# A feed-forward layer in two phases: the whole first product through DRAM, then the second, both in the seven-product form

## The chip, the cores and the metric

One core of a Trainium2 chip runs the whole program. The metric is the device time of one execution in microseconds, as the median of several runs; lower is better. A profiled execution gives, beside it, the span from the first to the last instruction and a trace of every instruction.

## The reference, cut to what matters

Causal attention over 4 batches, 12 heads, 448 positions and head size 64 makes x of 4 x 448 rows and 768 columns. A Fourier mix is added, the rows are normed, and two products with a ReLU between them make the feed-forward layer:

```python
X = np.fft.fft(np.fft.fft(x, axis=1), axis=2)
u = x + np.real(X)
un = (u - mean(u)) / np.sqrt(var(u) + 1e-06)
ch = np.maximum(un @ w_ch1, 0.0) @ w_ch2     # 768 -> 3072 -> 768
return u + ch
```

## The kernel before, in words

The work is cut into units by `tile_kernel`. Each unit has an engine (or a choice of engines), a cost, a priority and the tiles that it reads and writes. `Plan.order` is a list scheduler in Python: it always takes the unit that can start first by its own model, and so writes out one fixed order for every engine. The table `LEADS` shifts the priority of single units. All DMAs are issued by SyncE, in that order. Tiles live in pools ("A1", "A2", "Q", "E1", "E2", "L") that share memory: a pool opens when those named in `AFTER` have seen their last use.

Attention (`attend`, 24 pairs of heads) and the Fourier part (`fold`, `dft`, by batch) come first. `dft` writes u to the DRAM tensor `ud` and the transposed, normed un to `und`.

The 1792 rows of un form two groups of 896 (two batches each), and the 3072 middle columns 12 chunks of 256. An item is one group and one chunk; the 24 items run group by group. For each, `f1` makes the first product for the chunk and `f2` adds the second one to the sums `acc0` to `acc6`, which stay in SBUF for the whole group. The `f1` of one item and the `f2` of the item before it are interleaved on TensorE.

Every factor is split into a high and a low fp32r part, and a product takes three matmuls: high by high, high by low, low by high. A 2 x 2 product of blocks takes eight block products in the plain form, and seven in the other form (named `fast` for `f1`, `seven` for `f2`), which needs sums and differences of blocks first (`mixed`, `halves`, `quarters`, `hblocks`).

- `f1`, matmuls of 128x448: the items of group 0 with chunk 0 to 2 are plain (4 outputs, 18 matmuls each: 72). The other 21 items take 7 products of 9 matmuls (63).
- `f2`, matmuls of 128x384: ten items of group 0 are plain (line 1484: 7 row tiles, 2 halves, 6 matmuls: 84). The other fourteen, chunks 4 and 6 of group 0 (`STR`) and all of group 1, are seven-product (line 1445: 7 steps x 3 row tiles x 3 matmuls, and 12 matmuls for the seventh, middle row tile that has no partner: 75).

After each product of three matmuls (six in a plain item) VectorE adds the PSUM bank to `acc` (line 1433). In the seven-product form a bank runs through several steps, and the next step in it waits for that addition. In `f1` a pass runs through seven products, copies three of them to `c` tiles (`keep`, line 611), adds on VectorE (`plus`, line 1314) and applies ReLU (line 1263).

Weights are read in `weights` with their layout of bits undone by three ScalarE operations (lines 989, 993, 1006) and two of VectorE (1012, 1016) per 128 rows; `halves` and `quarters` split them (high part line 611, low part 1066 and 1126). Group 1 reads `w1` parts that group 0 left in DRAM (`wp`).

## Time and profile before

| | us |
|---|---|
| median of 3 runs | 899.98 |
| lowest and highest | 898.37, 901.57 |
| span of the profiled execution | 896.1 |
| median less span | 3.9 |
| TensorE busy in the profile | 879.0 |

The page of the profile gives each engine's busy time over the span; a table of stretches gives the same for chosen parts of it, also for the instructions of one line alone. The durations of matmuls in the trace overlap, since they are pipelined.

### The profile page before, as it was taken

Reading aid. Unit: us, or ns where it says so; the run is one execution under the profiler, and the core shown is the slowest. Engines: PE = TensorE matmul, PEld = TensorE weight load, DVE = VectorE, ACT = ScalarE, POOL = GpSimd, SP = SyncE. Lnnn points to the kernel's source line nnn. Section 1 sums busy time; section 2 is a strip of 40 time slices with the busy share of each in tenths; the row PEclk is TensorE's granted clock in tenths of the full one; section 3 lists DMA queues with packets and bytes.
Section 4 is the critical chain, followed back from the end, with each engine's and each line's share of the span. In section 5 each row is a group of like instructions: output and inputs, shape, how many; then the busy total and the mean of one; then the engine's idle time right before and its main releaser. Section 6 shows DMA issues by size and latency. Waiting matters only on the chain.

```text
span 896.1 us, 15887 instructions
## 1 busy us (share of the span) xinstructions
PE 879.0 (98%) x5560; PEld 785.3 (88%) x5560; DVE 682.1 (76%) x1281; ACT 595.1 (66%) x1258; POOL 512.2 (57%) x596
## 2 busy tenths in 40 slices
PE   8999999999999999999999999999999999999998
PEld 4676686676889999999999999999999999999998
DVE  5868979868987988999999888867535445755748
ACT  6889998958675887989877568554534334544452
POOL 1564645735323230313135223889997969899996
PEclk9999999999999999999999999999999999999999
DMA  6456656324589565876698685764363344244113
GB/s 253 137 166 200 183 192 190 113 68 130 169 276 324 195 270 199 291 286 244 230 343 316 242 269 179 272 230 148 106 211 119 132 141 152 93 125 157 37 53 124
DMA packets 70081, 169.52 MB, mean 189 GB/s; under 512 B 19184, under 2 KB 31984, under 8 KB 70000
## 3 DMA queue, kind: packets, MB, share of 16 engines
q1 hardware_dynamic: 70000, 168.50, 56.1%
q8 instruction: 44, 0.72, 0.3%
q14 instruction: 37, 0.30, 0.1%
HBM read 112.63 MB, written 55.84 MB: 188 GB/s over the span
## 4 chain that ended last, share of the span: by engine, by line
PE 76%; DVE 10%; POOL 5%; ACT 4%; DMA 3%; issue 2%; SPq 0%; DVEq 0%; ACTq 0%; POOLq 0%
PE psum L1240 29%; PE psum L1445 17%; PE psum L1484 14%; PE psum L779 4%; PE psum L713 4%; PE psum L789 4%; PE psum L850 2%; DVE acc L1433 2%; ACT p L733 1%; DVE mn L725 1%; PE psum L706 1%; DVE w L1016 1%; DMA us<-und 1%; POOL w L1137 1%; PE psum L938 1%
## 5 line engine op out<-in xcount | busy, mean ns | idle before, releaser
L1433 DVE TENSOR_TENSOR acc<-psum,acc 128x384 f32<-128x384 f32 x462 | 243.9, 553 | 100.1 <-PE psum L1445 83.4
L1484 PE MATMUL psum<-w2h,hh 128*128 128x384 f32 x280 | 94.5, 338 | 0.9 <-ACT us L1263 0.6
L1006 ACT ACTIVATE w<-w 128x768 int8<-128x768 f32 x48 | 94.3, 1964 | 0.4
L1484 PE MATMUL psum<-w2l,hh 128*128 128x384 f32 x280 | 94.4, 337 | 0.0
L1484 PE MATMUL psum<-w2h,hl 128*128 128x384 f32 x280 | 94.2, 337 | 0.0
L733 ACT ACTIVATE p<-psum,mn 128x128 f32<-128x128 f32 (+3 forms) x168 | 82.8, 518 | 12.7 <-DVE mn L725 8.3
L1033 POOL TENSOR_TENSOR w2l<-w,w2h 128x768 fp32r<-128x768 f32 x20 | 40.3, 2026 | 74.4 <-ACT w2h L1029 63.8
L1445 PE MATMUL psum<-w2h,hh 128*128 128x384 f32 x336 | 73.0, 338 | 0.0
L1445 PE MATMUL psum<-w2l,hl 128*128 128x384 f32 x336 | 70.2, 339 | 0.1
L725 DVE TENSOR_REDUCE mn<-psum 128x1 f32<-128x448 f32 (+3 forms) x96 | 61.4, 665 | 10.9 <-PE psum L713 10.6
L767 POOL TENSOR_TENSOR p<-p,ri 128x128 f32<-128x128 f32 (+3 forms) x62 | 34.1, 572 | 62.3 <-DVE ri L745 52.4
L1314 DVE TENSOR_TENSOR c<-psum,c 128x448 f32<-128x448 f32 x63 | 38.7, 617 | 39.1 <-PE psum L1240 27.4
L713 PE MATMUL psum<-raw,qs 64*128 64x128 f32 (+3 forms) x336 | 66.6, 430 | 1.6 <-DMA cd<-in_cd_dram 1.1
L1445 PEld LDWEIGHTS psum<-w2h,hh 128*128 128x128 f32 x336 | 60.5, 188 | 1.4
L1445 PEld LDWEIGHTS psum<-w2l,hl 128*128 128x128 f32 x336 | 59.7, 188 | 1.6 <-DVE acc L1433 0.4
L779 PEld LDWEIGHTS psum<-cst,p 128*128 128x128 f32 x384 | 42.5, 141 | 19.8 <-issue 9.4
L1240 PE MATMUL psum<-u12h,w 128*128 128x448 f32 x162 | 59.3, 368 | 0.2 <-DVE acc L1433 0.2
L1240 PE MATMUL psum<-u21h,w 128*128 128x448 f32 x162 | 59.2, 368 | 0.1
L1240 PE MATMUL psum<-u11h,w 128*128 128x448 f32 x162 | 58.8, 368 | 0.2 <-DVE w L1066 0.2
L1240 PE MATMUL psum<-u22h,w 128*128 128x448 f32 x162 | 58.7, 368 | 0.0
L611 ACT CAST w2h<-w 128x384 fp32r<-128x384 f32 x56 | 28.4, 513 | 45.5 <-PE psum L1445 22.9
L779 PE MATMUL psum<-cst,p 128*128 128x128 f32 x384 | 52.8, 278 | 3.5 <-POOL p L767 2.3
(171 smaller groups left out, 2526.9 us busy)
## 6 DMA issues: line engine op xcount, KB each, us to landing
...
us<-und SPq DMA_DIRECT2D x45, 224.0 KB, 4.1
...
```

Of the source, the lines that this page charges most:

```text
L713: nc.tensor.matmul(out=T[ps][:, at[r]:at[r] + n], lhsT=T[qs][s, q0:q0 + 128], rhs=T[raw][s, QW:QW + n], start=False, stop=y == len(rows) - ...
L725: nc.vector.tensor_reduce(out=z, in_=x, axis=AX, op=ALU.min)
L733: nc.scalar.activation(out=T[pb][:, PO[rr]:PO[rr] + n], in_=T[ps][:, c0:c0 + n], func=ACTF.Exp, scale=-1.0, bias=T[mn][:, rr:rr + 1], accu ...
L779: nc.tensor.transpose(T[ps][:, 128 * k:128 * k + 128], T[pb][:, e:e + 128], T["cst", 0][:, 0:128])
L789: nc.tensor.matmul(out=T[xps][64 * h:64 * h + 64, q0:q0 + w], lhsT=T[v][:, c, h * D:(h + 1) * D], rhs=T[pa][:, s0 + h * sd:s0 + h * sd + w ...
L1006: nc.scalar.activation(out=T[w].bitcast(I8)[:, :, 3], in_=T[w][:, :, 1].bitcast(F32), func=ACTF.Prelu, scale=SIGN_SCALE, alpha=SIGN_ALPHA)
L1033: nc.gpsimd.tensor_tensor(out=T[wl], in0=T[w32].bitcast(F32), in1=T[wh], op=ALU.subtract)
L1240: nc.tensor.matmul(out=T[ps][:, 0:S], lhsT=a[:, t], rhs=x[:, t], start=start and k == 0, stop=stop and k == 8, skip_group_check=True)
L1314: nc.vector.tensor_tensor(out=T[z], in0=T[ps][:, 0:S], in1=T[z], op=ALU.add)
L1433: nc.vector.tensor_tensor(out=x, in0=T[ps][:, 0:384], in1=x, op=ALU.add)
L1445: nc.tensor.matmul(out=T[ps][:, 0:384], lhsT=hpart(j, h, a)[:, k * 128:k * 128 + 128], rhs=T[z][:, 384 * b:384 * b + 384], start=start and ...
L1484: nc.tensor.matmul(out=T[ps][:, 0:384], lhsT=T[a][:, m, k * 128:(k + 1) * 128], rhs=w[:, sl], start=(m == 0 and z == 0), stop=(m == 1 and ...
```

## The change

The feed-forward layer no longer runs item by item. First all of the first product runs, and its ReLU output goes to a DRAM tensor `h`; then the second product runs, and reads `h` back.

- First phase: chunks 0 to 2 for group 0 alone (`ALONE`), chunks 3 to 11 for both groups step by step in turn, then chunks 0 to 2 for group 1 alone, with w1 read again from DRAM. Every pass is in the seven-product form: 24 passes of 63 matmuls.
- Second phase: a window is one pair of row tiles, tile i of group 0 with tile i of group 1, and three chunks (`WIN`): 7 steps of 9 matmuls that sum over the three chunks in one PSUM bank before VectorE adds the bank to the sum. There are 7 x 4 = 28 windows. The sums of all 14 row tiles stay in SBUF.
- The pieces of w2 are made once for each chunk, 7 of the 12 chunks in the first phase (`EARLY`), which go to DRAM and come back (`fetch`).
- The U blocks of group 0 are mixed while attention still runs (`build`): u11 and u21 stay in SBUF tiles of their own (`EDGE`), the others go through DRAM (`td`) and are split in `refill`. The U blocks of group 1 are built in a pool that opens after "Q".
- Buffers: 3 `p` buffers of attention (4 before), 2 `w` (3), 5 `w32` (4), 8 `w1` tiles (7), 4 `us` (5). PSUM: up to 4 banks for each group's first product and 8 for the second (5 and 5 before).
- A new table `PICK` fixes the engine of many units, and `LEADS` has new values throughout.

```diff
-N_RAW, N_V, N_QK, N_W, N_W32, N_PA, N_RB = 4, 4, 2, 3, 4, 2, 2
+N_RAW, N_V, N_QK, N_W, N_W32, N_PA = 4, 4, 2, 2, 5, 2
 F1_CUT = 3
+ALONE, WIN, REST, EARLY, JOIN = 3, 3, (0,) * 7, (0, 3, 5, 6, 8, 9, 11), ()
+W1_LEAD, W1_LEAD2, W2_LEAD, H_LEAD, W2_FROM, W2_TILL, FETCH_LEAD = 1200, 1500, 2600, 600, 3000, 5000, 2000
+BUILD_AT = (19000, 300)
-BANKS = dict(sc=(1, 3), sd=(1, 2), pt=(1, 3), x=(1, 2), ay=(1, 3), an=(1, 1), at=(1, 5), h=(0, 5), o2=(0, 5))
-N_P, N_XT, N_Y, N_F, N_D = 4, 1, 1, 1, 1
-AFTER = dict(E1=("A1",), E2=("A1", "A2"), L=("Q",))
+BANKS = dict(sc=(1, 3), sd=(1, 2), pt=(1, 3), x=(1, 2), ay=(1, 3), an=(1, 1), at=(1, 5), h0=(0, 4), h1=(0, 4), o2=(0, 8))
+N_P, N_XT, N_Y, N_F, N_D = 3, 1, 1, 1, 1
+AFTER = dict(E0=("A1",), E2=("A1", "A2"), L=("Q",), F=("E2",), G=("L",))
+BELOW = dict(E2=("E0",))
...
+UB = ("11", "21", "t2", "t1", "t3", "22", "t4")
+W1B = ("11", "12", "s2", "s1", "s3", "s4", "22")
+W2B = ("11", "21", "t2", "t1", "t3", "22", "t4")
+HB = ("x0", "x1", "s2", "s1", "s3", "s4", "y1")
+STEPS = (
+    ("x0", "11", "a", 0, 0, True, False), ("x1", "21", "d", 0, 0, True, True), ("s2", "t2", "a", 0, 1, False, False),
+    ("s1", "t1", "b", 1, 1, True, False), ("s3", "t3", "a", 1, 1, False, False), ("s4", "22", "b", 0, 1, False, True),
+    ("y1", "t4", "a", 1, 0, False, True))
...
+    def build(g, p0):
+        ph = "E" if g else "Q"
+        for k in range(3):
+            p = p0 + (30 if g else 300) * k
+
+            def minus(name, x, y, rd=()):
+                plan.part("minus", g, k, name)
+                into = y if name in ("t1", "t3") else x
+                return combine(S, into[0], x, y, ALU.subtract, (*into[1][0][:2], name), p + 2, ph, rd)
+
+            def put(name, src):
+                if g or name in EDGE:
+                    return usplit(g, name, k, src, p + 3, ph)
+                plan.part("td", k, name)
+
+                def f(k=k):
+                    nc.sync.dma_start(out=dr["td"][UB.index(name)][:, k], in_=src[0]())
+                add("D", dma(229376), p + 3, f, rd=src[1], wr=[("td", name, k)], phase=ph)
+                return [("td", name, k)]
+            plan.part("slabs", g, k)
+            b11 = slab(g, 0, k, 1, p, ph)
+            b12 = slab(g, 1, k, 1, p, ph)
+            b22 = slab(g, 1, k + 3, 1, p, ph)
+            b21 = slab(g, 0, k + 3, 1, p, ph)
+            d11 = put("11", b11)
+            t1 = minus("t1", b12, b11, d11)
+            put("t1", t1)
+            d22 = put("22", b22) if g else []
+            t3 = minus("t3", b22, b12, t1[1])
+            put("t3", t3)
+            t2 = minus("t2", b22, t1, [*d22, *t3[1]])
+            put("t2", t2)
+            d21 = put("21", b21)
+            t4 = minus("t4", b21, t2, d21)
+            put("t4", t4)
...
+    FLOW = (
+        ("11", "11", "a", True, False), ("12", "21", "d", True, True), ("s2", "t2", "a", False, False), ("s1", "t1", "b", True, False),
+        ("s3", "t3", "a", False, False), ("s4", "22", "b", False, True), ("22", "t4", "a", False, True))
+    place = {c: k for k, c in enumerate([*range(ALONE, NCH), *range(ALONE)])}
+
+    def f1(c, gs, again, p0):
+        step = 143 * len(gs)
+        bank, kept = {}, {}
+        for s, (wn, un, x, first, last) in enumerate(FLOW):
+            for y, g in enumerate(gs):
+                plan.part("f1", c, g, s)
+                p = p0 + step * s + 143 * y
+                ps = ("h%d" % g, (c, x))
+                wb = ("w1", ((c, again), wn))
+                us = [utile(g, un, t) for t in range(3)]
+                dep = [] if first else [kept["u2", g][1]] if wn == "s3" else [kept["m1", g][1]] if wn == "s2" else \
+                    [kept["u3", g][2]] if wn == "s4" else [kept["u3", g][1]]
+                for q in range(F1_CUT):
+                    ks = range(9 * q // F1_CUT, 9 * (q + 1) // F1_CUT)
+                    ts = sorted({k // 3 for k in ks})
+
+                    def f(ks=ks, ps=ps, wb=wb, us=us, first=first, last=last):
+                        w = T[wb]
+                        for k in ks:
+                            t, z = divmod(k, 3)
+                            a, b = ((0, 0), (0, 1), (1, 0))[z]
+                            nc.tensor.matmul(
+                                out=T[ps][:, 0:S], lhsT=w[:, a, t], rhs=T[us[t]][:, b], start=first and k == 0, stop=last and k == 8,
+                                skip_group_check=True)
+                    add("PE", len(ks) * mm(S) + 19 / F1_CUT, p + q, f,
+                        rd=[(*wb, "h"), (*wb, "l"), *[(*us[t], z) for t in ts for z in "hl"], *dep,
+                            *([(*ps, s, q - 1)] if q else [])],
+                        wr=[(*ps, s, q)], phase="E")
+                done = (*ps, s, F1_CUT - 1)
...
+                def out_(z, key, m, n, p, g=g):
+                    def f():
+                        nc.sync.dma_start(out=dr["h"][m, g][:, place[c], n * S:(n + 1) * S], in_=T[z])
+                    add("D", dma(229376), p - 1500, f, rd=[key], wr=[("hd", m, g, c, n)], phase="E")
+
+                def keep(name, ps=ps, done=done):
+                    z = ("us" if again and name == "m1" else f"c{g}", (c, name, again))
+
+                    def f(eng):
+                        copy(eng, T[z], T[ps][:, 0:S])
+                    add(("S", "V"), (act(448), dve(448)), p + 143, f, rd=[done], wr=[(*z, 0)], phase="E")
+                    kept[name, g] = [z, (*z, 0)]
+
+                def plus(name, m, n, ps=ps, done=done):
+                    z = kept[name, g][0]
+
+                    def f():
+                        nc.vector.tensor_tensor(out=T[z], in0=T[ps][:, 0:S], in1=T[z], op=ALU.add)
+                    add("V", dve(448), p + 144, f, rd=[done, (*z, 0)], wr=[(*z, 1)], phase="E")
+                    kept[name, g].append((*z, 1))
+                    relu(z, lambda: T[z], [(*z, 1)], (acts(448), dve(448, 1.92)), m, n)
+
+                def relu(z, src, rd, cost, m, n):
+                    def f(eng):
+                        if eng == "S":
+                            nc.scalar.activation(out=T[z], in_=src(), func=ACTF.Relu)
+                        else:
+                            nc.vector.tensor_scalar(out=T[z], in0=src(), scalar1=0.0, scalar2=None, op0=ALU.max)
+                    add(("S", "V"), cost, p + 145, f, rd=rd, wr=[(*z, 2)], phase="E")
+                    out_(z, (*z, 2), m, n, p)
+
+                if wn == "11":
+                    keep("m1")
+                elif wn == "12":
+                    plus("m1", 0, 0)
+                elif wn == "s2":
+                    keep("u2")
+                elif wn == "s1":
+                    kept["b", g] = (ps, done)
+                elif wn == "s3":
+                    keep("u3")
+                    plus("u3", 1, 1, *kept["b", g])
+                elif wn == "s4":
+                    plus("u2", 0, 1)
+                else:
+                    z = (f"c{g}", (c, "c21", again))
+                    relu(z, lambda ps=ps: T[ps][:, 0:S], [done], (act(448), dve(448)), 1, 0)
...
+    def slice_(k, name):
+        return ("wa" if (7 * k + W2B.index(name)) % (N_WA + N_WB) < N_WA else "wb", (k, name))
...
+    def window(i, k0, k1, p0):
+        order = [*range(ALONE, NCH), *range(ALONE)]
+        n, id_ = k1 - k0, ("h", i, k0)
+        w = 128 * n
+        ns = sorted({(i * 128) // S, (i * 128 + 127) // S})
+        raw = {}
+        plan.part("raw", i, k0)
+        c, c_ = ("c0", "c1") if len(seen) == 1 else (f"c{len(seen) % 2}",) * 2
+        seen.append(id_)
+        for name, tag, m, g in (("y0", c, 0, 1), ("y1", c_, 1, 1), ("x0", "us", 0, 0), ("x1", "us", 1, 0)):
+            z = (tag, (id_, name))
+
+            def f(z=z, m=m, g=g):
+                nc.sync.dma_start(
+                    out=T[z][:, 0:w].rearrange("p (c t) -> p c t", c=n), in_=dr["h"][m, g][:, k0:k1, i * 128:i * 128 + 128])
+            add("D", dma(512 * w), p0 - 1000, f, rd=[("hd", m, g, order[k], q) for k in range(k0, k1) for q in ns], wr=[z], phase="L")
...
+        bank = {x: ("o2", (id_, x)) for x in "abd"}
+        for s, (h, wn, x, row, half, first, last) in enumerate(STEPS):
+            plan.part("f2", i, k0, s)
+            ps, hb, acc = bank[x], ("w1", (id_, h)), acc_(i + NT * row)
+            p = p0 + 94 * n * s
+            ws = [slice_(k, wn) for k in range(k0, k1)]
+
+            def f(ps=ps, hb=hb, ws=ws, first=first, last=last):
+                for y, z in enumerate(ws):
+                    for v, (a, b) in enumerate(((0, 0), (0, 1), (1, 0))):
+                        nc.tensor.matmul(
+                            out=T[ps][:, 0:384], lhsT=T[hb][:, a, y], rhs=T[z][:, b], start=first and y + v == 0,
+                            stop=last and y == n - 1 and v == 2, skip_group_check=True)
+            add("PE", 3 * n * mm(384) + 8, p, f, rd=[(*hb, "h"), (*hb, "l"), *[(*z, v) for z in ws for v in "hl"],
+                *([] if first else [(*ps, "v")])], wr=[(*ps, s)], phase="L")
+
+            def f(ps=ps, k=i + NT * row, half=half):
+                x = whole(k)[:, half * 384:(half + 1) * 384]
+                nc.vector.tensor_tensor(out=x, in0=T[ps][:, 0:384], in1=x, op=ALU.add)
+            add("V", dve(384) + 4, p + 94 * n, f, rd=[(*ps, s), (*acc, half)], wr=[(*acc, half), (*ps, "v")], phase="L")
...
+    at(-9000, build, 0, BUILD_AT[0])
+    at(-800, refill, F0 - 800)
+    at(BUILD_AT[1], build, 1, F0 + BUILD_AT[1])
+    for c in range(NCH):
+        t = 1000 * c if c < ALONE else 1000 * (2 * c - ALONE)
+        at(t - W1_LEAD - 200, w1s, c, False, F0 + t - W1_LEAD)
+        at(t, f1, c, (0,) if c < ALONE else (0, 1), False, F0 + t)
+        if c < ALONE:
+            t = 1000 * (2 * NCH - ALONE + c)
+            at(t - W1_LEAD2, w1s, c, True, F0 + t - W1_LEAD2)
+            at(t, f1, c, (1,), True, F0 + t)
+    t, last, gate = 2000.0 * NCH, [0] * NT, []
+    for k in range(NCH):
+        if k not in EARLY:
+            at(t - W2_LEAD, w2s, k, F0 + t - W2_LEAD)
+        else:
+            x = W2_FROM + (2000.0 * NCH - W2_TILL - W2_FROM) * EARLY.index(k) / len(EARLY)
+            at(x, w2s, k, F0 + x)
+            at(t - W2_LEAD, fetch, k, F0 + t - FETCH_LEAD + (30 * k if k < WIN else 0))
+        for i in range(NT):
+            if k == NCH - 1 or (k + 1) % WIN == REST[i]:
+                if not last[i]:
+                    for row in range(2):
+                        at(t - H_LEAD, total, i + NT * row, F0 + t, gate[-2:-1])
+                    gate.append((f"c{len(gate) % 2}" if len(gate) != 1 else "c0", (("h", i, last[i]), "y0")))
+                at(t - H_LEAD, window, i, last[i], k + 1, F0 + t)
+                t += 282 * (k + 1 - last[i])
+                if k == NCH - 1:
+                    for row in range(2):
+                        at(t - H_LEAD, store, i + NT * row, F0 + t)
+                last[i] = k + 1
+    for _, _, fn, args in sorted(todo, key=lambda x: x[:2]):
+        fn(*args)
```

## Rows read from the trace of the kernel before

**Rows 1.** The page: the span; busy time, share and instructions of each engine
```profile
span 896.1 us, 15887 instructions
PE 879.0 (98%) x5560; PEld 785.3 (88%) x5560; DVE 682.1 (76%) x1281; ACT 595.1 (66%) x1258; POOL 512.2 (57%) x596
```

**Rows 2.** Stretches: from:to, length, busy time of each engine (instructions), clock, DMA
```profile
227.00:300.00 73.00, 71.86 (x385) 65.50 (x384) 61.28 (x100) 48.99 (x75) 24.35 (x24) 1.00 0.74 248
300.00:475.00 175.00, 173.73 (x920) 164.92 (x919) 168.26 (x312) 149.31 (x216) 44.84 (x37) 1.00 0.74 265
300.00:875.00 575.00, 573.63 (x3053) 549.14 (x3052) 423.08 (x765) 353.16 (x628) 365.04 (x382) 1.00 0.57 194
```

**Rows 3.** The chain that ended last, in order of time: start, length, what
```profile
266.77 18.27 PE psum L1240 x90
...
485.89 24.98 PE psum L1484 x144
```

**Rows 4.** The same stretches, line 1240 alone (PE, PEld)
```profile
227.00:300.00 73.00, 47.44 (x216) 39.63 (x216) 1.00 0.74 248
300.00:475.00 175.00, 94.34 (x414) 76.77 (x415) 1.00 0.74 265
300.00:875.00 575.00, 297.86 (x1323) 245.48 (x1323) 1.00 0.57 194
```

**Rows 5.** The same stretches, line 1484 alone
```profile
227.00:300.00 73.00, 11.49 (x66) 11.62 (x67) 1.00 0.74 248
300.00:475.00 175.00, 67.17 (x356) 62.30 (x354) 1.00 0.74 265
300.00:875.00 575.00, 145.41 (x776) 136.26 (x774) 1.00 0.57 194
```

**Rows 6.** The same stretches, line 1445 alone
```profile
300.00:475.00 175.00, 31.24 (x150) 26.64 (x150) 1.00 0.74 265
300.00:875.00 575.00, 185.10 (x954) 169.60 (x955) 1.00 0.57 194
```

**Rows 7.** Groups of instructions: count, busy time, mean ns, idle time before
```profile
L1006 ACT ACTIVATE w<-w 128x768 int8<-128x768 f32 x48 | 94.3, 1964 | 0.4
L1016 DVE SCALAR_TENSOR_TENSOR w<-w,w 128x768 uint32<-128x768 uint32 x48 | 46.6, 973 | 3.0 <-ACT w L1006 2.8
L1314 DVE TENSOR_TENSOR c<-psum,c 128x448 f32<-128x448 f32 x63 | 38.7, 617 | 39.1 <-PE psum L1240 27.4 <-ACT c L611 11.1
L611 ACT COPY c<-psum 128x448 f32<-128x448 f32 x61 | 32.7, 542 | 34.4 <-PE psum L1240 29.6 <-POOL hh L1372 4.6
L1066 DVE TENSOR_TENSOR w<-w,w 128x384 fp32r<-128x384 f32 x37 | 24.5, 679 | 5.3 <-ACT w L611 5.2
L1066 POOL TENSOR_TENSOR w<-w,w 128x384 fp32r<-128x384 f32 x11 | 11.6, 1057 | 25.5 <-ACT w L611 16.5 <-DVE w L613 7.4 <-issue 1.6
```

**Rows 8.** Instructions of PE in order of time: start, length, what
```profile
227.01 0.47 PE L1240 MATMUL psum<-u11h,w 128*128 128x448 f32 x1
...
266.03 0.74 PE L938 MATMUL psum<-cst,un 112*128 112x112 f32 x6
```

**Rows 9.** DMA issues: count, KB each, median us from issue to landing
```profile
us<-und SPq DMA_DIRECT2D x45, 224.0 KB, 4.1
und<-ub SPq DMA_DIRECT2D x32, 168.0 KB, 3.0
```

**Rows 10.** Instructions of DVE in order of time: start, length, what
```profile
271.04 0.38 DVE L613 CAST t3h<-us 128x448 fp32r<-128x448 f32 x1
271.34 2.04 DVE L613 CAST t2h<-us 128x448 fp32r<-128x448 f32 x1
```

**Rows 11.** Instructions of POOL in order of time, the same moment
```profile
271.26 3.84 POOL L1033 TENSOR_TENSOR w2l<-w,w2h 128x768 fp32r<-128x768 f32 x2 [6.66 <-ACT w2h L1029]
```

**Rows 12.** The stretch from the start to 102.4, line 733 alone (ACT)
```profile
0.00:102.40 102.40, 43.95 (x169) 1.00 0.60 191
```

**Rows 13.** The stretch from the start to 99.4, line 779 alone (PE, PEld)
```profile
0.00:99.40 99.40, 22.13 (x163) 18.19 (x164) 1.00 0.59 190
```

1032 lines of the change are left out of this document (423 added, 609 removed), and 1791 rows, old and new, of tables (LEADS, PICK).

## The prediction

> **What bounds the kernel now.** The page comes first: TensorE is called busy for 98% of the span, every other engine for 57 to 76% [rows 1]. The durations behind that 98% overlap, so I read the true rate from the chain of waits in order of time, where long runs of one line stand unbroken: 90 matmuls of line 1240 in 18.27 us, 0.203 us each, and 144 of line 1484 in 24.98 us, 0.1735 us each [rows 3]. Line 1445 has the same shape and I give it the same price. Then the table of stretches, by line, shows how densely these stand. From 300 to 875 there are 1323 matmuls of 128x448 and 776 + 954 of 128x384 [rows 4 to 6], and no others, for the sum is the stretch's own count of 3053 [rows 2]. At those rates they need 268.6 + 300.2 = 568.8 of 575 us: 6.2 us, 1.1%, is lost. In the hardest part, 300 to 475, VectorE is busy for 168 of 175 us and ScalarE for 149 [rows 2], and 414 + 506 matmuls need 171.8 us [rows 4 to 6]: 3.2 us lost, 1.8%. So the feed-forward part is bound by the number of matmuls and by nothing else, even where two other engines are nearly full. The clock is 1.00, the 2.4 GHz level, in all three stretches [rows 2].
>
> The way into it is looser. The first matmul of line 1240 stands at 227.01, and the last of the Fourier part at 266.03 [rows 8]. From 227 to 300 there are 216 of line 1240 and 66 of line 1484 [rows 4, 5], 43.8 + 11.5 = 55.3 of 73 us. The other 17.7 us are 103 matmuls (385 less 282 [rows 2]) of the Fourier part, and waits.
>
> **The change part by part.** *First product.* Before: 3 items of 72 and 21 of 63 matmuls, 1539. After: 24 passes of 63, 1512. 27 x 0.203 = **5.5 us less**.
>
> *Second product.* Before: 10 items of 84 and 14 of 75, 1890. After: 28 windows of 63, 1764. 126 x 0.1735 = **21.9 us less**. That a bank now sums nine matmuls in place of three changes neither their number nor their shape. VectorE's additions fall from 462 to 196, but VectorE isn't on the path, so this is worth nothing by itself. It also loosens a wait: in a window, the step that reuses a bank has one whole step, 9 x 0.1735 = 1.56 us, between itself and the one whose sum VectorE must read first; before, s3 followed s2 in bank "a" with two products of three matmuls between, 1.04 us.
>
> *Density.* I let the 1.1% stand, so it is worth nothing either way. The lower bound is the whole 6.2 us given back; the upper one is the 1.8% of the hardest stretch for all 613 us of matmuls, 4.3 us more than now. The load of a two-group chunk (126 x 0.203 = 25.6 us) supports it: every chunk needs two halves of w1 and, for 7 of 12 chunks in that phase, w2 too, which the schedule spreads at about 0.9 w2 chunk per w1 chunk. That is 3.8 runs of the bit operations; the dearest takes 1.96 us on ScalarE and the dearest 0.97 us on VectorE [rows 7]. Some 21 low parts and differences at 0.68 us on VectorE or 1.06 us on GpSimd [rows 7], six copies at 0.54 us and six additions at 0.62 us [rows 7] come to less than 25.6 us on each engine if GpSimd takes half of the low parts.
>
> *The way in.* This is new work at a tight place. Let the 17.7 us of others stay as they are: three passes of group 0 alone are 189 x 0.203 = 38.4 us, so they end at 227 + 38.4 + 17.7 = 283.1, and group 0's pass of chunk 3 at 295.9. Group 1 needs its U blocks by then. They go into pool "L", which opens after the Fourier part. Its last matmul is at 266.8 [rows 8], the write of und lands 3.0 us later and a slab takes 4.1 us more [rows 9]: 273.9. There are 12 slabs and 4 buffers, so three rounds, each with one landing and a chain of some eight operations in series (split, t1, t3, t2, t4, split) at about 0.68 us: 4.1 + 5.4 = 9.5 us. The first product needs u11 of the third round, 273.9 + 2 x 9.5 + 4.1 + 1.4 = 298.4, 2.5 us after PE has run dry. Taken: **3 us more**. Bounds: below nothing by 4, if the two products on u11 and u21 (18 x 0.203 = 3.7 us) that need no new pool fill waits before 227; 15 us above, if the three rounds don't overlap with the refill of group 0, which takes 15 more slabs through the same four buffers (four landings of 4.1 us).
>
> *Attention.* The mixing of group 0 adds 12 differences, 12 halves of splits and DMAs to its last fifth; GpSimd is at 57% over the span [rows 1] and can hide them. The fourth `p` buffer goes. At the tightest place that I found, the thirteenth pair's first exponential has just begun at 102.4 (12 pairs of 14 instructions, and 1 [rows 12]) while the tenth pair's 16 transposes were over by 99.4 (163 of line 779, 160 are needed [rows 13]): with three buffers it would have been free. Taken: 0. Bounds: 4 us either way, as the engines are assigned anew.
>
> *Between the phases.* The windows begin with chunks 3 to 5, whose rows of `h` were written long before. 17 slices of w2 have a pool ("wa") that opens when group 0 is done, 38 us ahead. Only four blocks of the third slice must wait for the last matmul of the first phase; the first of them is needed after three steps, 4.7 us, and takes a high and a low part, about 0.7 + 1.06 us [rows 7]. Covered. SyncE's queue holds the raw reads of the next windows behind the fetches of w2; if one is late, it costs a landing, 4.1 us [rows 9]. Taken: **1 us more**, bounds 0 and 5. At the very end the last addition and the last store stay: 0.
>
> **Sum:** -5.5 - 21.9 + 3 + 1 = -23.4 us. The span of 896.1 becomes 872.7; the median lies 3.9 us above the span, so **876.6 us**.
>
> **The rivals.** *A shared port.* At 271.34 a cast on VectorE took 2.04 us where its twin took 0.38 [rows 10], while GpSimd had begun a two-input subtraction at 271.26, two of which took 3.84 us [rows 11]: one engine stood while the other worked. On the way in, low parts and differences of chunks 1 to 3 (33), of the refill (15) and of group 1 (33) stand in 227 to 296. If they never overlap between the two engines, they take 81 x 0.68 + 6 x 0.97 = 60.9 us when all are VectorE's, and 0.38 us more for each that GpSimd takes: 76 us at 40 of them. VectorE has the Fourier part's own work too and must give some away. About 76 us against 68.9 us of PE's work is 7 us more than forecast: **883 us**. The Trainium skill, "SBUF — State Buffer", section "Who interferes with whom", speaks against the change here: a VectorE instruction with two SBUF inputs and a GpSimd one that reads SBUF exclude each other. The cast above agrees as to exclusion. Against the rival: work for chunk 1 can stand before 227.
>
> *A lucky way in.* The 18 matmuls before 227, no wait for group 1 and none between phases: 876.6 - 3.7 - 3 - 1 = **869 us**.
>
> *The evacuation chain of the first phase (slower).* Within a pass, s3's bank is copied (0.54 us), b's bank is added to the copy (0.62 us) [rows 7], and only then may s4 go into b. In the two-group phase only the other group's product, 9 x 0.203 = 1.83 us, lies between, and the second product no longer stands there to fill. If ScalarE's queue has a 1.96 us operation and VectorE's a 0.97 us one in front [rows 7], the chain is 4.1 us and the pass loses 2.3 us, or all 4.1 in the six single-group passes: 18 x 2.3 + 6 x 4.1 = 66 us at worst. It turns the gain into a loss from 23.4 / 24 = 1 us for each pass; at half its worst, 33 us, the time is **910 us**. Against it: the same chain ran 21 times before beside a VectorE at 96%, with 1.8% lost in all; the t4 product needs only the copy; and each group has a fourth bank, so the next chunk's first product can step in.
>
> That the change doesn't do what it says can't be here: the counts follow from the loops.
>
> **How the numbers follow.** Forecast 0.56, shared port 0.18, lucky way in 0.14, evacuation chain 0.12, of which 0.07 is slower, 0.03 within 0.3% and 0.02 still faster. A measurement of this kernel can tell about 0.3% (2.7 us) from no change. So faster 0.90, same 0.03, slower 0.07. The range takes in 869 less the 4 us of attention and 883 with the 4.3 of density and the 5 of the phases: 865 to 892. It leaves out the worse end of the way in and most of the chain.
>
> **What would show it.** In the trace after: 1512 and 1764 matmuls at 0.203 and 0.1735 us; 196 additions into the sums; the first-product phase starting near 227 and its last matmul near 227 + 17.7 + 307 + 3 = 555; unbroken chains on TensorE in both phases. Wrong would be: waits of TensorE on copies in 300 to 550 (chain), VectorE and GpSimd operations at twice their price near 270 to 300 (port), attention that ends some us off 227, or any fall of the granted clock after a pause between the phases.

## The result and the profile after

| | before | after |
|---|---|---|
| median of 4 runs, us | 899.17 | 888.40 |
| lowest and highest | 897.56, 901.57 | 886.11, 891.54 |
| profiled execution, its span | 896.1 (span) | 887.22, 885.4 |
| forecast | | 876.6 (865 to 892) |

The ratio is 0.9884 (95% interval 0.9856 to 0.9912). The change is faster by 10.8 us, where 23.4 were forecast: the sign and the range held, and half of the gain is missing. The page of the profile after, first part (busy time and instructions of each engine), answers to [rows 1]:

```profile
PE 856.2 (97%) x5407; PEld 758.5 (86%) x5407; DVE 745.5 (84%) x1458; ACT 531.4 (60%) x1094; POOL 327.6 (37%) x355
```

In the file after, line 2802 makes the first product, 2979 the second, 2987 VectorE's additions to the sums, 2655 low parts, 2661 sums and differences of blocks, 2262 and 2264 copies and casts, 2461 to 2478 the Fourier fold, 2440 the last step of attention; in the files of the experiments the same lines stand some lines lower. The table of stretches after, all engines (columns: stretch, its length, busy time and count of PE, PEld, DVE, ACT, POOL, granted clock, DMA share, GB/s), beside [rows 2]:

```profile
0.00:227.00 227.00, 219.05 (x2019) 156.91 (x2021) 190.42 (x415) 194.06 (x556) 110.10 (x164) 0.98 0.58 186
227.00:300.00 73.00, 62.56 (x331) 52.99 (x332) 67.73 (x126) 57.27 (x105) 24.04 (x25) 0.98 0.64 200
300.00:525.00 225.00, 224.74 (x1101) 205.84 (x1100) 183.23 (x325) 170.84 (x242) 53.60 (x47) 1.00 0.81 273
525.00:575.00 50.00, 46.45 (x230) 42.05 (x229) 42.13 (x82) 33.95 (x55) 17.00 (x15) 1.00 0.76 250
575.00:612.00 37.00, 34.53 (x192) 32.81 (x192) 36.32 (x71) 15.62 (x30) 8.86 (x7) 1.00 0.86 285
612.00:882.30 270.30, 268.87 (x1543) 267.88 (x1541) 225.40 (x446) 59.62 (x108) 113.97 (x97) 1.00 0.44 140
```

and line 2802 alone in the first four of them (PE, PEld, clock, DMA share, GB/s):

```profile
0.00:227.00 227.00, 4.91 (x18) 3.00 (x18) 0.98 0.58 186
227.00:300.00 73.00, 47.19 (x199) 36.39 (x200) 0.98 0.64 200
300.00:525.00 225.00, 224.74 (x1101) 205.84 (x1100) 1.00 0.81 273
525.00:575.00 50.00, 41.22 (x198) 36.28 (x196) 1.00 0.76 250
```

Read them with the two rates of the forecast, 0.203 and 0.1735 us. From 300 to 525 there are 1101 matmuls, 223.5 of 225 us: 0.7% lost. From 612 on 1543 x 0.1735 = 267.7 of 270.3: 1%. Both phases are as dense as forecast. Three places are not. From 227 to 300 only 199 x 0.203 = 40.4 of 73 us are feed-forward work, where there were 55.3 before. From 525 to 575, 198 x 0.203 + 32 x 0.1735 = 45.7 of 50 (4.3 lost), and from 575 to 612, 192 x 0.1735 = 33.3 of 37 (3.7 lost). The waits of TensorE, from the list of waits (what it waited for: us in total, times, longest), say on what, first for 227 to 300 and then for 525 to 612:

```profile
PE psum L2802 <- DVE 0t L2655: 5.4, 3, 4.7
PE psum L2802 <- ACT c L2262: 1.4, 2, 0.8
PE psum L2802 <- DVE 1211_3676 L2655: 1.1, 1, 1.1
PE psum L2802 <- DVE w L2655: 0.9, 1, 0.9
PE psum L2802 <- DVE c L2264: 0.7, 1, 0.7
...
PE psum L2802 <- DVE c L2264: 1.9, 1, 1.9
PE psum L2802 <- ACT c L2262: 1.7, 1, 1.7
PE psum L2979 <- ACT w L2262: 1.1, 1, 1.1
PE psum L2979 <- DVE acc L2987: 1.0, 1, 1.0
```

The longest is one wait of 4.7 us. The timeline of 228 to 240 (start, us, engine, line, tiles; in brackets the idle time before and what ended it) on GpSimd, ScalarE, VectorE and TensorE:

```profile
229.09 2.57 POOL L2661 TENSOR_TENSOR ws<-w,ws 128x384 f32<-128x384 f32 x1 [4.84 <-DVE w L2655]
231.62 2.59 POOL L2461 TENSOR_TENSOR d<-xt 128x448 f32<-128x448 f32 x2
231.69 0.51 ACT L2262 CAST w<-ws 128x384 fp32r<-128x384 f32 x1 [1.22 <-POOL ws L2661]
...
232.65 0.56 DVE L2655 TENSOR_TENSOR w<-w,w 128x384 fp32r<-128x384 f32 x1 [1.86 <-ACT w L2262]
...
234.24 0.62 DVE L2471 TENSOR_TENSOR o<-d 128x446 f32<-128x446 f32 x1 [1.03 <-POOL d L2461]
234.94 0.62 DVE L2471 TENSOR_TENSOR e<-d 128x446 f32<-128x446 f32 x1
235.48 0.55 DVE L2655 TENSOR_TENSOR w<-ws,w 128x384 fp32r<-128x384 f32 x1
235.65 1.83 POOL L2478 TENSOR_TENSOR f<-e 128x226 f32<-128x226 f32 x2 [0.74 <-DVE e L2471]
235.95 2.01 DVE L2655 TENSOR_TENSOR 0t<-us,0t 128x448 fp32r<-128x448 f32 x2
...
237.05 2.24 PE L2802 MATMUL psum<-0t,w 128*128 128x448 f32 x5 [4.73 <-DVE 0t L2655]
239.09 2.14 PE L2501 MATMUL psum<-cd,f 128*111 128x194 f32 x9
```

GpSimd takes 2.57 us for one sum of w1 blocks (a sum of the same shape took 1.02 us at 251.04). Only then come the first steps d of the last Fourier fold. VectorE's o waits for d, and the low part 0t, for which TensorE waits, stands behind o in VectorE's queue. VectorE is not short of time at this point: it stands idle for 1.86 us, for a cast in ScalarE's queue behind the cast of GpSimd's sum, and for 1.03 us, for d. And the pause costs twice. The same 16 us in slices of 4 (columns as in the first table; clock third from the end):

```profile
228.00:232.00 4.00, 3.02 (x30) 2.32 (x26) 2.79 (x7) 2.49 (x7) 2.91 (x2) 1.00 0.15 39
232.00:236.00 4.00, 0.33 (x2) 0.00 (x0) 2.24 (x5) 3.94 (x8) 3.20 (x4) 1.00 0.20 75
236.00:240.00 4.00, 2.95 (x8) 2.63 (x9) 4.00 (x6) 0.92 (x2) 3.33 (x4) 0.59 0.35 79
240.00:244.00 4.00, 4.00 (x25) 3.83 (x24) 4.00 (x8) 1.42 (x4) 0.00 (x0) 0.99 0.64 170
```

After TensorE was busy for 0.33 of 4 us the granted clock fell to 0.59, mostly the 1.2 GHz level, for the next 4. Before, these four slices have a clock of 1.00, and TensorE is never busy for less than 3.25 of 4 us in them.

**The balance.** Feed-forward matmuls: -27.3 us (1512 and 1764, counted). What else fills the time up to 300: before 300 - 55.3 = 244.7, after 300 - 217 x 0.203 = 255.9, so +11.2; of this 2.2 are attention, whose last matmul stands at 228.68, and stood at 226.45 before (line 789 there), and 9.0 the way in (+3 forecast). Lost from 300 to TensorE's end: 13.1 where it was 7.1, +6.0 (+1 forecast). The tail: -0.6. Together -10.7, the difference of the two spans.

### The profile page after: what moved, and what is told of

It reads as the page before. It is cut to its first block, busy times and chain, and to the rows that moved or that the text cites. A ratio compares the mean times of both kernels' runs of the same rounds, so it can differ in the third digit from the quotient of the medians.

```text
span 885.4 us, 15855 instructions
## 1 busy us (share of the span) xinstructions
PE 856.2 (97%) x5407; PEld 758.5 (86%) x5407; DVE 745.5 (84%) x1458; ACT 531.4 (60%) x1094; POOL 327.6 (37%) x355
## 4 chain that ended last, share of the span: by engine, by line
PE 56%; DVE 8%; issue 2%; ACT 2%; DMA 1%; POOL 0%; DVEq 0%; ACTq 0%; POOLq 0%
PE psum L2979 30%; PE psum L2802 27%; DVE w L2655 2%; DVE ue L2987 1%; DMA acc<-ud 1%; DMA w<-in_w_dram 1%; DVE w L2639 1%; ACT w L2629 1%; DVE c L2828 0%; DVE acc L2987 0%; DVE us L2661 0%; DVE w L2661 0%; DVE ws L2661 0%; DVE w L2264 0%; DVE c L2838 0%
## 5 line engine op out<-in xcount | busy, mean ns | idle before, releaser
L2979 PE MATMUL psum<-wa,w 128*128 128x384 f32 x1050 | 210.5, 337 | 3.6 <-DVE acc L2987 1.8
L2979 PEld LDWEIGHTS psum<-wa,w 128*128 128x128 f32 x1050 | 184.9, 188 | 6.0 <-ACT w L2262 3.0
L2979 PE MATMUL psum<-wb,w 128*128 128x384 f32 x714 | 148.7, 334 | 0.0
L2979 PEld LDWEIGHTS psum<-wb,w 128*128 128x128 f32 x714 | 125.4, 188 | 0.0
L2802 PE MATMUL psum<-0t,w 128*128 128x448 f32 x432 | 111.5, 372 | 8.1 <-DVE 0t L2655 5.4
L2802 PE MATMUL psum<-1t,w 128*128 128x448 f32 x432 | 105.4, 365 | 3.5 <-DVE c L2264 1.9
L2802 PEld LDWEIGHTS psum<-0t,w 128*128 128x128 f32 x432 | 80.8, 189 | 17.4 <-DVE 0t L2655 6.4
L2802 PEld LDWEIGHTS psum<-1t,w 128*128 128x128 f32 x432 | 80.5, 188 | 12.4 <-ACT c L2262 2.8
L2987 DVE TENSOR_TENSOR acc<-psum,acc 128x384 f32<-128x384 f32 x112 | 61.0, 552 | 30.9 <-PE psum L2979 30.3
L2655 POOL TENSOR_TENSOR w<-ws,w 128x384 fp32r<-128x384 f32 x30 | 33.3, 1116 | 101.5 <-ACT w L2262 66.5
L2262 ACT CAST w<-us 128x384 fp32r<-128x384 f32 x47 | 23.8, 519 | 70.8 <-PE psum L2979 42.5
L2430 PE MATMUL psum<-cst,p 128*128 128x128 f32 x384 | 55.3, 283 | 5.2 <-POOL p L2418 3.6
L2802 PE MATMUL psum<-ue,w 128*128 128x448 f32 x216 | 55.6, 373 | 0.3 <-DVE w L2655 0.3
L2987 DVE TENSOR_TENSOR ue<-psum,ue 128x384 f32<-128x384 f32 x84 | 46.1, 551 | 10.5 <-PE psum L2979 9.8
```

Of the source, the lines that this page charges most:

```text
L2262: nc.scalar.copy(out=out, in_=in_)
L2430: nc.tensor.transpose(T[ps][:, 128 * k:128 * k + 128], T[pb][:, e:e + 128], T["cst", 0][:, 0:128])
L2655: (nc.gpsimd if eng == "G" else nc.vector).tensor_tensor(out=lo(), in0=src(), in1=hi(), op=ALU.subtract)
L2802: nc.tensor.matmul(out=T[ps][:, 0:S], lhsT=w[:, a, t], rhs=T[us[t]][:, b], start=first and k == 0, stop=last and k == 8, skip_group_check= ...
L2979: nc.tensor.matmul(out=T[ps][:, 0:384], lhsT=T[hb][:, a, y], rhs=T[z][:, b], start=first and y + v == 0, stop=last and y == n - 1 and v == ...
L2987: nc.vector.tensor_tensor(out=x, in0=T[ps][:, 0:384], in1=x, op=ALU.add)
```

## The experiments

Three theories. *Theory 1, work*: on the way in and between the phases passes of one group alone give TensorE half the matmuls for each w1 block, while VectorE and ScalarE also make U blocks or w2 pieces; too much work for too little time. *Theory 2, hand-over and order*: the right operation is late (copy, addition, next product; landings; the place in a queue), not too much of it. *Theory 3, the shared port*: VectorE and GpSimd shut each other out.

To keep the disturbance of one stretch out of the next, all runs are read at the same marks, counted in order of time on TensorE: A the last matmul of attention, B the 701st of the first product, C the 1201st, E the 301st of the second product, F its last. B to C was 102.6 to 102.7 us in all runs but the last of the cut ones.

| run | A | clock, 227 to 300 | A to B | C to E | E to F | time |
|---|---|---|---|---|---|---|
| changed kernel | 228.7 | 0.98 | 170.2 | 123.9 | 256.2 | 888.4 |
| e12, the same again | 227.8 | 0.95 | 171.4 | 123.9 | 256.2 | 888.5 |
| e1 no U low parts | 226.7 | 0.98 | 167.4 | 123.9 | 256.2 | 882.5 |
| e2 w bits cut, way in | 229.8 | 0.95 | 171.1 | 123.9 | 256.2 | 889.3 |
| e3 all cut, way in | 227.4 | 0.98 | 162.1 | 123.9 | 256.2 | 878.2 |
| e4 w2 cut, between | 226.2 | 0.95 | 171.3 | 120.9 | 256.7 | 883.1 |
| e5 no w1 low parts | 226.7 | 0.95 | 166.8 | 123.9 | 256.2 | 881.6 |
| e6 additions cut, between | 226.7 | 0.95 | 171.1 | 124.7 | 256.2 | 887.0 |
| e7 all cut, between | 227.9 | 0.95 | 171.5 | 119.1 | 256.7 | 882.2 |
| e8 all cut | 230.4 | 0.98 | 162.2 | 119.1 | 254.5 | 873.4 |
| e9 eleven units moved | 226.5 | 0.91 | 175.9 | 122.7 | 256.8 | 890.1 |
| e10 fold on VectorE | 228.2 | 0.98 | 168.0 | 123.9 | 256.2 | 885.5 |
| e11 e10 and four more | 226.4 | 0.98 | 167.2 | 123.8 | 256.3 | 884.5 |

The clock is the granted one of TensorE. Where nothing on the way in was changed, A to B is 170.2 at a clock of 0.98 (the changed kernel) and 171.1 to 171.5 at 0.95 (e4, e6, e7, e12), in the same program; so each run is held against those at its own clock. A shorter wait may itself keep the clock up, so this is the cautious comparison. One profile stands behind each number, and only one behind the 170.2. Times of e1, e2, e4, e5 and e6 are of one execution, the others medians of 4.

**What the cut runs share.** They keep the changed kernel's order; a unit named by `no_low` makes no low part, and the matmul reads the high one; a unit named by `is_thin` handles an eighth of its columns.

```diff
-        def f(eng):
+        def f(eng, name=plan.name):
+            if no_low(name):
+                return
             (nc.gpsimd if eng == "G" else nc.vector).tensor_tensor(out=lo(), in0=src(), in1=hi(), op=ALU.subtract)
...
                             a, b = ((0, 0), (0, 1), (1, 0))[z]
+                            a *= not no_low(("block", (c, again), wn))
+                            b *= not no_low(("put", g, t, un))
...
+            thin.on = is_thin(u["group"][0], u["group"][1], plan.start[u["n"]] / 1e3)
             u["fn"](*([u["eng"]] if u["many"] else []))
+            thin.on = False
```

**e1**, `no_low`: `name[0] == "put"`.

> The order of all instructions stays as in the changed kernel; left out is the low part of every U block of both groups (the subtraction of line 2655 for them), and the matmuls read the high part in its place, as many as before. In the changed kernel the last matmul of the first product starts at 570.81, and 217 of its matmuls stand before 300. Theory 1, work: from 227 to 300 VectorE (67.7 of 73 us busy) and ScalarE (57.3) are full with preparing blocks for passes of one group alone, which give TensorE little, so TensorE waits for blocks. About 40 subtractions of 0.5 us fewer on VectorE and GpSimd give back the waits on them (5.4 us on group 0's low parts, some 2 on group 1's): last matmul at 563 to 566, about 245 matmuls before 300. Theory 2, hand-over: TensorE waits in these passes for the copy of a bank, the addition and the landings through four buffers, one after the other, and VectorE's load is beside the point: 569 to 571, at most 225 before 300. Theory 3, the port that VectorE and GpSimd share: as theory 1 for the operations that GpSimd does itself, but few of them stand there: 568 to 570.

Measured: the last matmul of the first product at 566.02, 240 of them before 300; A to B 167.4, 2.8 less than the changed kernel at the same clock. The 566.02 lies where theory 1 put it, but 2.0 us of it come from attention, which ended earlier; without them it is 568.0, between theory 1 and the two others. And the wait at 232 did not go. It passed to what stands behind it: TensorE now waited 4.1 us for the fold's last step f, which GpSimd makes (line 2478 of the changed kernel).

**e2**, `is_thin`: `weights`, the operations on bits, by chunk.

> Left out are seven eighths of each of the four operations that undo the layout of bits (lines 2616 and 2629 on ScalarE, 2635 and 2639 on VectorE) for the weights that pass from 227 to 300 (w1 of half of chunk 2, of chunks 3 and 4, and w2 of chunk 3): about 13 us less on ScalarE and 6 us less on VectorE in that stretch. Theory 1 (work on VectorE and ScalarE): last matmul of the first product at 566 to 569 in place of 570.81. Theory 2 (hand-over): 569.5 to 571, since no wait of TensorE ends on these lines by itself.

Measured: 572.82, and A to B 171.1, no gain, although from 227 to 300 ScalarE was busy for 46.7 us in place of 57.3 and VectorE for 62.4 in place of 67.7. Its stretch of 227 to 300, and the waits on group 0's low parts:

```profile
227.00:300.00 73.00, 62.64 (x331) 53.04 (x330) 62.35 (x126) 46.69 (x103) 22.51 (x25) 0.95 0.63 199
...
PE psum L2836 <- DVE 0t L2689: 5.4, 3, 4.7
```

The long wait is as long as before. So ScalarE's load on the way in is not the cause, and 5.4 us less of VectorE's work are worth nothing either where that work does not stand in front of what TensorE waits for.

**e3**, both, with `block` of chunks 0 to 4 in `no_low` and the additions and ReLUs in `is_thin` (the copies stayed whole, other than the text on record says).

> Both of the above, and also without the low parts of the w1 blocks of chunks 0 to 4, and with an eighth of the copies, additions and ReLUs that empty the first product's banks from 227 to 300. What then remains of the loss on the way in is neither of the engines' load: landings, the order itself and the Fourier part. Theory 1 (work): TensorE's losses of 227 to 300 fall by 8 us or more: last matmul of the first product at 558 to 563, time about 878 to 880. Theory 2 (landings through four buffers and the written order): 566 or later, time 883 or more.

Measured: 561.50 and 878.23 us, ratio to the kernel before 0.9798 (0.9758 to 0.9838): theory 1. Its stretch of 227 to 300, and all that TensorE still waited for there by the list of waits:

```profile
227.00:300.00 73.00, 68.75 (x366) 61.79 (x363) 38.37 (x86) 50.66 (x114) 11.82 (x18) 0.98 0.70 231
...
PE psum L2539 <- POOL f L2516: 2.2, 1, 2.2
PE psum L2844 <- ACT c L2300: 1.1, 2, 0.6
PE psum L2844 <- DVE c L2302: 0.7, 1, 0.7
```

With VectorE at 38.4 us in place of 67.7, 8.0 us of A to B are back against the changed kernel at the same clock; left are the fold's chain and the bare hand-over of a bank, 0.6 to 0.7 us each.

**e4**, `no_low`: `slice` (w2 pieces not made in the first phase); `is_thin`: the bits of w2 of chunks 5, 7 and 10.

> Between the phases: left out are the low parts of the w2 pieces that are not made in the first phase, and seven eighths of the four operations on bits for w2 of chunks 5, 7 and 10. In the changed kernel TensorE loses 4.3 us of 525 to 575 and 3.7 of 575 to 612. Theory 1 (work: VectorE 36.3 of 37 us busy in 575 to 612): the 3.7 us shrink below 1, and of the 4.3 a half goes: from 525 to TensorE's last matmul 351 to 353 us in place of 357.0. Theory 2 (hand-over in the passes of one group alone, and one late read at 595): 355.5 to 357.

Measured: C to E 120.9, 3.0 less, of which 0.5 is lost again behind E. The part before 575 came as theory 1 said; the 3.7 us of 575 to 612 did not shrink below 1 but to 2.8 (197 x 0.1735 = 34.2 of 37), so w2's pieces are not what holds TensorE there.

**e5**, `no_low`: `block` of chunks 0 to 4.

> The order of the changed kernel, without the low parts of the w1 blocks of chunks 0 to 4 (25 subtractions of about 0.5 us from 227 to 300, 22 of them on VectorE); their matmuls read the high part. Counted from the last matmul of attention to the 701st of the first product, so that what attention's clock did to a run stays out: 170.2 us in the changed kernel, 171.1 and 171.3 in the two runs at a clock of 0.95 in 227 to 300, 167.4 without the U low parts, 162.1 without all of them and with cut additions. Theory 1 (VectorE's work on the way in): these weigh as much as the 40 of the U blocks or nearly so: 167 to 168.5. Theory 2 (what is left over is hand-over of banks): 169.5 to 171.

Measured: 166.8, 4.3 to 4.7 less than the runs at the same clock, slightly more than theory 1 said and more than the 40 operations of e1 gave. The longest wait up to 300 is 1.48 us, at 229.59. So VectorE's subtractions on the way in do count, those of the w1 blocks as well as those of U; with e2 beside it, that holds for these subtractions and not for VectorE's busy time as such.

**e6**, `is_thin`: additions and ReLUs of 500 to 575.

> The order of the changed kernel; from 500 to 575 seven eighths of each addition and ReLU that empties the first product's banks are left out (the copies stay whole). TensorE's two longest waits before the second phase, 1.8 us at 548.5 and 2.0 at 552.5, end on a copy of a bank. Theory 1 (work): little, the copies are late because of what stands before them on ScalarE and VectorE (bits of w2, 1.97 us each): from the 1201st matmul of the first product to its last 68.5 to 69.3 us in place of 69.25. Theory 2 (hand-over, addition before copy before product): 65.5 to 67.5.

Measured: C to the last matmul of the first product 68.6 in place of 69.25, theory 1; C to E as a whole 124.7, since the clock was 0.95 from 575 to 612 in this run. The two waits on copies are not made by the additions before them.

**e7**, e4 and e6 together, and `no_low`: `hb` of the first four windows' first chunks.

> As the run without w2's low parts and bits, and also without the low parts of the first windows' blocks of h and with the cut additions and ReLUs of 500 to 575. The stretch from the 1201st matmul of the first product to the 301st of the second takes 123.9 us in the changed kernel and 120.9 in the run named; its matmuls alone need 312 x 0.203 + 300 x 0.1735 = 115.4. Theory 1 (work of VectorE and ScalarE): 116 to 118, time about 881 to 883. Theory 2 (landings of h and of the sums, and banks that wait for an addition): 119.5 or more, time 884 or more.

Measured: C to E 119.1, 4.8 less, 0.6 lost again behind E, time 882.22 (ratio 0.9824, 0.9810 to 0.9839). It lies between the two expectations; the stretches of 525 to 575 and 575 to 612:

```profile
525.00:575.00 50.00, 48.65 (x244) 44.63 (x243) 28.82 (x70) 23.75 (x55) 11.47 (x11) 1.00 0.82 276
575.00:612.00 37.00, 35.76 (x206) 35.44 (x206) 23.84 (x47) 15.44 (x35) 7.13 (x7) 1.00 0.87 286
```

VectorE falls from 42.1 and 36.3 us to 28.8 and 23.8, and TensorE gains 14 matmuls in each. Of the 8.5 us over the bare 115.4, 4.8 are work; 3.7 stay, among them two bank hand-overs of 0.6 and 0.7 and one wait of 1.2 on a cast of a block of h.

**e8**, all of it through the whole kernel.

> The order of the changed kernel with VectorE's and ScalarE's feed-forward work cut through the whole kernel: no low parts of U, w1, w2 or h blocks (but the pieces of w2 that the first phase makes), an eighth of the four operations on bits, of the differences of U blocks, and of the additions and ReLUs of the first product. All 1512 + 1764 matmuls stay. It asks whether the 27.4 us of the removed matmuls are there at all once these engines have time. Theory 1 (work): the losses on the way in and between the phases go, together 12 to 15 us: time 873 to 876. Theory 2 (hand-over, landings, written order): 880 or more.

Measured: 873.44 us, ratio 0.9716 (0.9693 to 0.9739), as theory 1 said. So the gain that the removed matmuls promise is there once VectorE and ScalarE have room: the time is 3.2 us below the forecast's 876.6. Not all of it is lost at the two borders: 0.8 us come from B to C and 1.7 from E to F.

**e9**, nothing left out; eleven units are placed by hand (not shown: lines 2461 and 2466 of the changed kernel name VectorE for this one fold).

```diff
+# unit, the unit that it goes ahead of (None: it keeps its place), its engine (None: as planned)
+TURNS = (
+    (1424, None, "V"), (1254, None, "V"), (1255, None, "V"), (1256, None, "V"), (1437, 1428, None),
+    (1687, 1560, None), (1581, 1577, None), (3092, 3041, None), (3099, 3049, "S"), (3198, 3359, None), (3288, 3284, None))
...
     seq = plan.order()
+    for n, ahead, eng in TURNS:
+        u = plan.units[n]
+        if ahead is not None:
+            seq.remove(u)
+            seq.insert(seq.index(plan.units[ahead]), u)
+        u["eng"] = eng or u["eng"]
```

> Nothing is left out: the changed kernel with eleven of its units at another place or on another engine, chosen from its trace, where a long wait of TensorE ends on an operation that could have run earlier. At 229 to 237: one sum of w1 blocks and the first stage of the last Fourier fold (line 2461 and the copy behind it) go from GpSimd, which was busy for 4.84 of 5 us there, to VectorE, which was idle for 3 of those 5, and a low part of a U block goes ahead of them. At 285 and 292 two low parts, at 548 and 552 two copies of banks, at 584 a sum of h blocks and at 607 an addition go ahead of work that nothing waited for. Theory 1 (amount of work): VectorE and ScalarE are full, so what goes ahead of one thing delays another; each wait moves to the next block and at most 2 us come back: from attention's end to the 701st matmul of the first product 169 to 170.5 us (170.2 in the changed kernel, 171.1 to 171.5 at the lower clock), from the 1201st to the 301st of the second product 123 to 124 (123.9), time 886 to 888. Theory 2 (hand-over and written order: the right work is late, not too much of it): 2.4 us at 232, 1.9 at 285 and 292 and 3.8 between the phases: 165 to 167 and 120 to 121, time 880 to 882.

Measured: 890.12 us (ratio 0.9917, 0.9895 to 0.9939), 1.7 above the changed kernel. A to B is 175.9, worse by 4.5 to 5.8: both theories missed. The timeline of GpSimd and TensorE, and two slices:

```profile
232.39 6.33 POOL L2484 TENSOR_TENSOR f<-e 128x226 f32<-128x226 f32 x2 [10.30 <-DVE e L2477]
...
239.34 2.90 PE L2507 MATMUL psum<-cd,f 128*111 128x194 f32 x8 [4.58 <-POOL f L2484]
...
232.00:236.00 4.00, 2.45 (x9) 1.44 (x8) 4.00 (x9) 2.05 (x5) 3.61 (x1) 0.81 0.48 130
236.00:240.00 4.00, 0.66 (x2) 0.64 (x3) 1.66 (x3) 0.00 (x0) 3.87 (x4) 0.62 0.78 244
240.00:244.00 4.00, 4.00 (x15) 3.88 (x14) 0.74 (x2) 0.94 (x2) 0.00 (x0) 0.53 0.61 204
```

This is theory 3 at work. With the fold's first steps on VectorE, VectorE ran from 228 to 237.66 without a pause, and the first of the four operations that GpSimd was left with (line 2484, two f<-e and two f<-o), from 232.39 to 238.14, took 5.75 us; the next three, with VectorE idle, took 0.62, 0.61 and 0.61. The Trainium skill, "SBUF — State Buffer", section "Who interferes with whom", says that a VectorE instruction with two SBUF inputs and a GpSimd one that reads SBUF exclude each other. This run agrees, and in it the exclusion lasted through nine VectorE instructions in a row. It need not: in the changed kernel the same four operations ran from 235.65 to 239.33, beside a VectorE without a pause, took 0.87 to 1.00 us each and took turns with VectorE's. What decides between the two is not shown. Nor is the wait longer than before, 4.58 us against 4.73; what makes A to B worse is for the most part the clock, 0.91 from 227 to 300, up to 0.07 x 73 = 5.1 us more than at 0.98 and 2.9 more than at 0.95. Between the phases the moved units gave 1.2 us and lost 0.6 again behind E; on 285 to 296 the waits only went to the next block, as theory 1 said.

**e10**, only the first five turns, and the fold's last step on VectorE, behind the step before it.

```diff
+    (1259, 1426, "V"), (1260, 1426, "V"), (1261, 1426, "V"), (1262, 1426, "V"))
```

> Nothing is left out. Of the run before only the part at 229 to 237 is kept, and the last stage of that fold (line 2478, four operations) goes to VectorE too, directly behind the stage before it. In the run before, GpSimd's first operation of that stage took 6.33 us for a pair (2 x 0.9 in the changed kernel) while VectorE ran without a pause from 232 to 238.7, TensorE stood 4.74 us for it, and the granted clock of 228 to 244 was 0.53 to 0.81. Theory 3 (the shared port, of which VectorE's stream keeps GpSimd out): with nothing left for GpSimd there, the wait is gone, and with it the fall of the clock: from attention's end to the 701st matmul of the first product 163.5 to 166 us (170.2 in the changed kernel, 175.9 in the run before), time 882 to 885. Theory 1 (VectorE's amount of work): the low parts that TensorE needs next now come 1.4 us later, and the wait moves to them: 168 to 171, time 886 to 889. In both, a clock of 1.00 from 240 on if no wait over 2 us is left, lower if one is.

Measured: A to B 168.0, 2.2 less than the changed kernel at the same clock, 3.1 to 3.5 less than the runs at 0.95, and 8 less than e9; 885.51 us (ratio 0.9864, 0.9836 to 0.9891). A to B stands at the lower edge of theory 1, the time between theory 3 and theory 1. VectorE was busier from 227 to 300 than in the changed kernel, 70.8 us against 67.7, so the gain is one of place and engine, not of less work. The wait on GpSimd is gone, and TensorE now waits for a low part of VectorE, as theory 1 said, but for 1.53 us; TensorE's row, two slices in which the clock is back at 236, 4 to 8 us earlier than in the changed kernel and in e9, and the stretch of 227 to 300:

```profile
236.42 0.67 PE L2808 MATMUL psum<-0t,w 128*128 128x448 f32 x2 [1.53 <-DVE 0t L2661]
...
232.00:236.00 4.00, 2.90 (x9) 2.25 (x7) 3.97 (x11) 3.39 (x6) 0.00 (x0) 0.69 0.48 141
236.00:240.00 4.00, 3.58 (x21) 3.54 (x22) 4.00 (x9) 0.91 (x2) 0.00 (x0) 1.00 0.46 128
...
227.00:300.00 73.00, 64.72 (x343) 55.18 (x339) 70.84 (x137) 58.91 (x108) 14.79 (x17) 0.98 0.67 209
```

**e11 and e12**, on one chip: e10 with one more low part ahead of the fold's last step and three of e9's turns between the phases; and the changed kernel as it is.

```diff
+    (1440, 1259, None), (3092, 3041, None), (3099, 3049, "S"), (3288, 3284, None))
```

> Nothing is left out. As the run before, and one more low part of a U block goes ahead of the fold's last stage, since TensorE stood 1.5 us for it there; between the phases two copies of banks and one addition go ahead as in the run before that. Theory of the port (way in): from attention's end to the 701st matmul of the first product 166 to 167.5 us (167.97 in the run before). Between the phases the two theories are as before: if VectorE and ScalarE are full there, at most 1 us of 123.9 comes back and a part is lost again behind it; if the order is at fault, 3 us. Time 882 to 886, 2 to 6 us below the changed kernel beside it.

> The changed kernel as it is, on the same chip as the run above, to compare the two directly: 886 to 891 us by all theories. From attention's end to the 701st matmul of the first product 170 to 171.5, from the 1201st to the 301st of the second product 123.9, and a granted clock below 1.00 once between 228 and 244, behind the wait at 232.

Measured: 884.51 (881.72 to 886.69) and 888.46 us (885.73 to 889.36), ratios 0.9853 (0.9835 to 0.9872) and 0.9884 (0.9863 to 0.9905); the intervals overlap a little, the medians differ by 4.0 us. A to B is 167.2 against 171.4, 4.2 us less with not one operation less; against the changed kernel at the clock of e11, 0.98, it is 3.0. C to E is 123.8 against 123.9. That does not show that order gives nothing between the phases: in e11 the clock fell there, after waits of 1.70 and 0.55 us at 546 and 547, and in e12 it did not (525 to 575, e11 first):

```profile
525.00:575.00 50.00, 47.07 (x227) 42.39 (x226) 43.35 (x83) 29.00 (x49) 14.95 (x13) 0.97 0.78 253
525.00:575.00 50.00, 46.45 (x231) 42.03 (x229) 42.16 (x82) 34.08 (x55) 17.01 (x15) 1.00 0.76 250
```

The fall took up to 0.03 x 50 = 1.5 us. e11 has the lowest median of all versions that compute everything.

## Why the prediction was half right

**The range** held partly by luck. Its upper end, 892, was built of the port's 7 us, 4.3 of density and 5 between the phases; the 888.4 came of 9.0 on the way in, 2.2 of attention and 6.0 behind 300, which lies outside its own bounds of 0 to 5.

**Counts, rates and density** held: -27.3 us, 0.7 and 1% lost in the two phases, 196 additions (112 and 84 by the groups of line 2987), no waits on copies from 300 to 525. So the rival of the evacuation chain falls for the two-group phase. In the passes of one group, where it was priced at up to 4.1 us a pass, its bare form is there: 0.6 to 0.8 us at a hand-over, and 1.7 and 1.9 us where VectorE and ScalarE had w2's work in front (0.6 and 0.7 in e7).

**Attention, 0**: right where the clock stayed. At a clock of 1.00 up to 227 it ended at 226.2 to 226.7 (e1, e4, e5, e6, e9, e11), as before; the other runs are below.

**The way in, +3**: measured +9.0. The step that failed is "let the 17.7 us of others stay as they are". It priced the arrival of group 1's blocks, which cost about what was said (waits of 0.95 and 1.15 us at 285 and 292, the first of them on a low part of w1), and took the rest of the stretch as given. But the Fourier part's last fold is a chain over GpSimd and VectorE. Before, TensorE had first-product work in hand while it ran; its longest wait there was 0.7 us, at 233.87. After, the U blocks for that work come by DRAM, their low parts stand in VectorE's queue between the steps of that chain, and GpSimd makes a sum of w1 blocks ahead of its first step, in 2.57 us. The wait is 4.7 us and the fall of the clock some 1.6 more (0.41 x 4 us; in e12 0.50 x 4 and 0.20 x 4, 2.8). The rest is the hand-overs at 272 to 278, 2.1 us. With group 1's 2.1 us these come to 10.5, 1.5 more than the 9.0; that difference was not traced. e10 and e11 give back 2.2 and 3.0 us at the same clock, 3.1 to 4.3 against the runs at 0.95, with no operation less. They move the chain and the sum to VectorE and a low part ahead, all at once, so they show that place and engine count, and not how much of it the port was. e1, e3 and e5 show that VectorE's low parts feed the wait; e2 shows that neither ScalarE's work on bits nor VectorE's does.

**The rival of the shared port** (7 us, 883) named something that is there, and priced it by amount, over all low parts. In the changed kernel four of VectorE's operations between 236 and 240 took 0.97 to 1.05 us in place of 0.55 to 0.61, and the fold's four steps beside them 0.87 to 1.00 in place of 0.61. That is some 3 us on both engines together. TensorE lost time where such operations stood in the chain that it waited for; how much of the 4.7 us is the port's was not separated. The cast with which the rival was argued has one SBUF input and is no case of the rule on two inputs that was put beside it.

**The lucky way in**: its first condition came true, 18 matmuls on u11 and u21 stand before 227, the first at 122.24. They cost attention nothing at a clock of 1.00, but they were part of the work that TensorE then lacked at 232; what they were worth in sum was not measured.

**Between the phases, +1**: measured +6.0 from 300 on, nearly all of it in 525 to 612. The step that failed is "covered". It looked at the third slice's four blocks and at one landing, and not at the load: group 1's three passes alone, with half the matmuls for each w1 block, are where w2 of the chunks left over and the first windows' blocks of h are made. VectorE is busy for 36.3 of 37 us. e7 gives 4.8 us of it to that work, of which 0.6 is lost again. Another order of the same work gave 1.2 us in e9, of which 0.6 was lost again, and 0.1 in e11, where the fall of the clock took up to 1.5; so order is worth less there than the amount of work, but not shown to be worth nothing. The first product's last matmul, forecast for 555, stands at 570.81: 2.2 of attention, 6.0 of the way in, 4.3 of its last three passes, 1.6 of the 0.7% from 300 to 525, and 1.6 for 9 matmuls of the second product ahead of it.

**Granted clock**: a fall was named among the signs that would make the forecast wrong, but behind a pause between the phases. It came on the way in, and no price stood for it.

What stays open, beside the port's share of the wait: how much of the 5 us on the way in that e11 leaves is the amount of VectorE's work and how much its shutting out of GpSimd, since the runs that cut the one also cut the other.
